# A linear-attention and gated-FFN kernel: k's product on GpSimd, paired score matmuls, one state multiply, and another order

## The chip, the cores and the metric

The kernel runs on one core of one Trainium2 chip. The metric is the device time of one execution in microseconds (us); the comparison uses the median over several runs. The engines are TensorE (PE, with its weight loads shown apart as PEld), VectorE (DVE), ScalarE (ACT), GpSimd (POOL) and SyncE (SP), which issues most of the DMAs.

## The reference

A recurrence over 768 steps for 4 batches and 8 heads of dimension 48, then an RMS norm and a gated feed-forward layer (384 to 1536 to 384) on all 3072 tokens.

```
state = zeros((B, H, D, D))                      # B, H, S, D = 4, 8, 768, 48
for t in range(S):
    cur = einsum('bhd,bhe->bhde', u[None] * kt, vt)
    y[:, :, t] = einsum('bhd,bhde->bhe', rt, state + cur)
    state = wt[:, :, :, None] * state + einsum('bhd,bhe->bhde', kt, vt)
x = y.transpose(0, 2, 1, 3).reshape(B * S, H * D)
xn = x / sqrt(mean(x * x, axis=-1) + 1e-06) * rms_g
g = xn @ w_gate
out = (g / (1 + exp(-g)) * (xn @ w_val)) @ w_out
```

## The kernel before, in words

The sequence is cut into six superblocks n = 0 to 5 of 128 steps; each has four pieces j = 0 to 3, one per batch. A piece fills the 128 partitions with its steps and has 384 columns, 8 heads of 48. The recurrence runs in chunked form: within a piece by masked score matrices, from one superblock to the next by a state.

One piece passes through these steps, which are Python functions of (n, j). `load_r`, `load_k`, `load_v`, `load_w` bring inputs (lines 213 and 226, on SP's queue). `ln` takes the logarithm of w (ScalarE). `cs_mm` forms cumulative sums of it by a matmul with a triangular mask into PSUM (L369), four one-column matmuls for the totals of the chunk, one per pair of heads (L372), and, in superblock 2, a second masked sum for k (L375). In superblocks 3 to 5 `cs_add` makes k's sum on VectorE from the first one (L380). Superblocks 0 and 1 share a wider load of w and have their own sums (L355 to L362). `exp_r` and `exp_k` take exponentials; they are in place in PSUM except in superblock 1, where they write SBUF. `w_tot` copies the exponentials of the totals to SBUF (L400). `r_mul` (L403) and `k_mul` (L408) multiply r and k by their factors on VectorE and write bf16. `rk_tr` transposes both: by PE and a ScalarE copy in superblocks 0 and 1 (`rk_pe`, L431), by one DMA transpose on SP's queue in 2 to 5 (L436). `q_mm` computes the scores of even heads (L449, partitions 0 to 47) and odd heads (L451, partitions 64 to 111) in alternating matmuls into two PSUM banks. `q_mask_e` masks the even half on VectorE (L456); `q_copy_o` copies the odd half on ScalarE (L460) and `q_mask_o` masks it on GpSimd (L467). `st_mm` (L477) and `st_new` (L483, L485) make the next state. `y_mm` (L494, L497) gives the output of the piece.

The diagonal term has steps of its own: `bonus_mul` is two GpSimd products (L414, L415), `bonus_sum` a VectorE reduction (L419), `bonus_v` a GpSimd product (L424), and `x_add` adds it to y (L502). `x_sq`, `x_rstd` and `xn_mul` form the norm (ScalarE; GpSimd L515 and L516 for the root; ScalarE L520). In superblocks 0 to 3 `xn_pe` and `xn_out` transpose it through PE (L531, L542); in 4 and 5 a DMA transpose (`xn_tr`, L525) and `xn_gain` (L546) do.

The feed-forward layer of superblock n then takes, for each of 12 slices f of the hidden dimension, `gate_mm` and `val_mm` (three matmuls of 128x512 each, L557, into the PSUM pools psA and psB), `silu` on ScalarE (L200, as all activations), `h_mul` on VectorE (L575), and for each batch `o_mm` (twelve matmuls, L620, into psQ), `o_out` (L627 on VectorE, L629 on ScalarE) and `out_dma` (L635).

`ORDER` is a list of some 1,090 steps, one word per step, such as `gate_mm.1.5`. The last lines of the kernel run through it and call the functions. Every engine executes its instructions in the order in which this list issues them, SP's queue included, so the list decides what stands behind what. While superblock n has its gate and val matmuls, the recurrence of n + 1 is woven between them. `warm` is a matmul on zeros with no reader, used in the first 30 us. PSUM has eight banks: two in psA, two in psB, four in psQ, each pool taken in turn.

Of the kernel before, what the change touches and what calls it, by code (L numbers as in the profile page):

```python
# [25 lines left out]
load_r.0.0 load_k.0.1 load_w.0.0 warm.15.0 warm.25.0 load_w.0.1 ln.0.0 warm.3.0 warm.14.0 warm.33.0 cs_mm.0.0 warm.17.0  # L26
warm.23.0 warm.28.0 load_v.0.0 load_w.0.3 cast_v.0.0 load_k.0.0 load_w.0.2 bonus_mul.0.0 load_r.0.1 bonus_mul.0.1
load_r.0.2 load_k.0.2 load_r.0.3 load_v.0.1 bonus_mul.0.2 ln.0.1 exp_r.0.0 r_mul.0.0 ln.0.3 exp_k.0.0 w_tot.0.0
k_mul.0.0 bonus_sum.0.0 warm.7.0 warm.6.0 cs_mm.0.1 exp_r.0.1 r_mul.0.1 load_k.0.3 bonus_mul.0.3 load_v.0.3 warm.32.0
warm.11.0 warm.24.0 warm.16.0 load_k.1.1 load_v.0.2 load_r.1.0 load_k.1.3 load_k.1.0 load_r.1.3 load_v.1.0 load_r.1.1  # L30
warm.2.0 warm.30.0 warm.10.0 warm.9.0 rk_pe.0.0 load_v.1.1 load_k.1.2 load_r.1.2 load_w.2.1 bonus_v.0.0 load_v.1.2
load_gv.0.1 load_w.2.0 load_v.1.3 st_mm.0.0 st_new.0.0 ln.0.2 exp_k.0.1 warm.31.0 k_mul.0.1 load_r.2.0 warm.21.0
load_k.2.1 load_w.2.2 load_v.2.1 load_k.2.0 rk_tr.0.0 cs_mm.0.2 exp_r.0.2 bonus_sum.0.1 w_tot.0.1 bonus_v.0.1
load_gv.0.0 r_mul.0.2 exp_k.0.2 k_mul.0.2 rk_pe.0.1 warm.8.0 rk_tr.0.1 q_mm.0.0 q_mask_o.0.0 cs_mm.0.3 warm.5.0
exp_r.0.3 r_mul.0.3 w_tot.0.2 exp_k.0.3 k_mul.0.3 load_w.2.3 load_k.2.2 load_r.2.1 rk_pe.0.2 warm.0.0 warm.12.0
q_mm.0.1 rk_tr.0.2 load_r.2.2 cs_mm.1.0 exp_r.1.0 warm.1.0 warm.20.0 warm.18.0 w_tot.0.3 q_mask_o.0.1 q_mask_e.0.1
rk_pe.0.3 warm.13.0 warm.26.0 warm.4.0 cast_v.0.1 exp_k.1.0 q_mask_e.0.0 y_mm.0.0 warm.22.0 warm.19.0 rk_tr.0.3
cast_v.0.2 cast_v.0.3 bonus_sum.0.2 bonus_sum.0.3 warm.27.0 x_add.0.0 warm.29.0 x_sq.0.0 load_r.2.3 r_mul.1.0 q_mm.0.2
q_mask_e.0.2 y_mm.0.1 cs_mm.1.1 x_rstd.0.0 exp_k.1.1 xn_mul.0.0 warm.35.0 x_add.0.1 q_mask_o.0.2 warm.34.0 q_mm.0.3
q_mask_e.0.3 x_sq.0.1 exp_r.1.1 x_rstd.0.1 load_k.2.3 y_mm.0.2 bonus_v.0.2 x_add.0.2 x_sq.0.2 xn_mul.0.1 x_rstd.0.2  # L40
xn_mul.0.2 q_mask_o.0.3 cs_mm.1.2 st_mm.0.3 st_mm.0.2 st_new.0.2 xn_pe.0.0 bonus_v.0.3 y_mm.0.3 x_add.0.3 load_gv.1.0
load_gv.1.1 bonus_mul.1.0 xn_out.0.0 xn_pe.0.1 xn_out.0.1 x_sq.0.3 x_rstd.0.3 xn_mul.0.3 xn_pe.0.2 xn_out.0.2 cs_mm.1.3
exp_r.1.3 exp_r.1.2 exp_k.1.3 xn_pe.0.3 st_new.0.3 k_mul.1.0 rk_pe.1.0 rk_tr.1.0 st_mm.0.1 xn_out.0.3 gate_mm.0.0
gate_mm.0.1 exp_k.1.2 q_mm.1.0 val_mm.0.1 k_mul.1.3 r_mul.1.3 silu.0.0 st_new.0.1 val_mm.0.0 rk_pe.1.3 q_mask_e.1.0
h_mul.0.0 k_mul.1.1 q_copy_o.1.0 silu.0.1 h_mul.0.1 gate_mm.0.2 silu.0.2 gate_mm.0.6 silu.0.6 val_mm.0.2 h_mul.0.2
bonus_sum.1.0 gate_mm.0.3 gate_mm.0.5 val_mm.0.3 silu.0.3 h_mul.0.3 cast_v.1.0 st_mm.1.0 gate_mm.0.9 st_new.1.0
silu.0.5 gate_mm.0.4 silu.0.9 r_mul.1.1 val_mm.0.5 h_mul.0.5 bonus_mul.1.3 gate_mm.0.7 rk_tr.1.3 cast_v.1.1 silu.0.4
val_mm.0.4 h_mul.0.4 st_mm.1.1 rk_pe.1.1 st_new.1.1 val_mm.0.9 val_mm.0.6 h_mul.0.6 r_mul.1.2 bonus_v.1.0 q_mask_o.1.0
y_mm.1.0 bonus_mul.1.1 k_mul.1.2 rk_tr.1.1 gate_mm.0.8 silu.0.8 silu.0.7 val_mm.0.7 h_mul.0.7 rk_pe.1.2 rk_tr.1.2
q_mm.1.1 q_copy_o.1.1 gate_mm.0.11 silu.0.11 load_wo.0.0 load_wo.2.0 q_mask_e.1.1 x_add.1.0 bonus_mul.1.2 load_wo.1.0  # L50
val_mm.0.8 h_mul.0.8 h_mul.0.9 q_mm.1.3 q_copy_o.1.3 q_mask_o.1.3 bonus_sum.1.3 q_mm.1.2 q_mask_e.1.2 q_copy_o.1.2
bonus_sum.1.1 gate_mm.0.10 val_mm.0.11 silu.0.10 val_mm.0.10 h_mul.0.10 bonus_sum.1.2 h_mul.0.11 q_mask_o.1.1 y_mm.1.1
x_sq.1.0 q_mask_o.1.2 cast_v.1.2 y_mm.1.2 bonus_v.1.1 x_add.1.1 o_mm.0.0 q_mask_e.1.3 ln.2.0 cs_mm.2.0 ln.2.1 cs_mm.2.1
bonus_v.1.2 x_add.1.2 o_out.0.0 out_dma.0.0 x_rstd.1.0 x_sq.1.1 cast_v.1.3 y_mm.1.3 st_mm.1.3 st_new.1.3 o_mm.0.1
bonus_v.1.3 x_rstd.1.1 x_add.1.3 exp_r.2.0 xn_mul.1.0 xn_pe.1.0 exp_k.2.1 k_mul.2.1 xn_mul.1.1 exp_r.2.1 w_tot.2.1
x_sq.1.2 x_rstd.1.2 r_mul.2.0 xn_out.1.0 w_tot.2.0 st_mm.1.2 st_new.1.2 o_mm.0.2 ln.2.2 cs_mm.2.2 x_sq.1.3 xn_mul.1.2
xn_pe.1.2 exp_k.2.0 k_mul.2.0 rk_tr.2.0 o_out.0.1 xn_pe.1.1 xn_out.1.1 xn_out.1.2 o_mm.0.3 exp_k.2.2 k_mul.2.2
load_v.2.0 r_mul.2.1 rk_tr.2.1 ln.2.3 x_rstd.1.3 exp_r.2.2 w_tot.2.2 xn_mul.1.3 xn_pe.1.3 xn_out.1.3 cs_mm.2.3
exp_r.2.3 r_mul.2.2 r_mul.2.3 w_tot.2.3 exp_k.2.3 k_mul.2.3 load_w.3.0 cast_v.2.1 st_mm.2.1 load_w.3.3 val_mm.1.1
gate_mm.1.1 silu.1.1 h_mul.1.1 o_out.0.2 load_v.2.2 rk_tr.2.3 load_v.4.3 rk_tr.2.2 load_v.2.3 load_k.3.1 load_r.3.1  # L60
o_out.0.3 out_dma.0.3 st_new.2.1 gate_mm.1.0 silu.1.0 val_mm.1.0 h_mul.1.0 bonus_mul.2.1 bonus_sum.2.1 gate_mm.1.5
silu.1.5 gate_mm.1.7 silu.1.7 val_mm.1.5 h_mul.1.5 bonus_mul.2.2 bonus_mul.2.0 bonus_v.2.1 gate_mm.1.3 silu.1.3
q_mm.2.0 q_mask_e.2.0 bonus_sum.2.2 q_mm.2.1 q_mask_e.2.1 gate_mm.1.2 silu.1.2 val_mm.1.2 h_mul.1.2 gate_mm.1.4
cast_v.2.0 st_mm.2.0 st_new.2.0 val_mm.1.3 h_mul.1.3 val_mm.1.4 gate_mm.1.6 bonus_mul.2.3 cast_v.2.2 st_mm.2.2
q_copy_o.2.1 bonus_sum.2.0 silu.1.4 h_mul.1.4 silu.1.6 q_copy_o.2.0 bonus_v.2.2 q_mask_o.2.0 q_mask_o.2.1 bonus_sum.2.3
cast_v.2.3 gate_mm.1.8 st_new.2.2 val_mm.1.7 gate_mm.1.9 h_mul.1.7 val_mm.1.9 y_mm.2.1 x_add.2.1 bonus_v.2.0 silu.1.9
h_mul.1.9 gate_mm.1.10 silu.1.10 y_mm.2.0 x_add.2.0 bonus_mul.3.1 val_mm.1.6 h_mul.1.6 q_mm.2.2 q_copy_o.2.2
q_mask_o.2.2 x_sq.2.0 q_mask_e.2.2 x_rstd.2.0 q_mm.2.3 q_mask_e.2.3 val_mm.1.8 val_mm.1.11 silu.1.8 h_mul.1.8
bonus_sum.3.1 bonus_v.2.3 q_copy_o.2.3 q_mask_o.2.3 load_r.3.0 load_k.3.0 bonus_mul.3.0 gate_mm.1.11 silu.1.11
h_mul.1.11 st_mm.2.3 y_mm.2.2 ln.3.0 val_mm.1.10 h_mul.1.10 o_mm.1.0 x_add.2.2 st_new.2.3 o_out.1.0 xn_mul.2.0 y_mm.2.3  # L70
x_add.2.3 cs_mm.3.0 xn_pe.2.0 cs_add.3.0 load_w.3.1 load_k.3.2 ln.3.1 cs_mm.3.1 cs_add.3.1 xn_out.2.0 out_dma.0.1
load_w.3.2 ln.3.2 x_sq.2.1 x_rstd.2.1 x_sq.2.2 load_k.3.3 out_dma.0.2 load_r.4.1 load_r.3.3 load_v.3.0 out_dma.1.0
load_v.3.2 load_r.3.2 exp_r.3.0 w_tot.3.0 bonus_sum.3.0 r_mul.3.0 ln.3.3 exp_k.3.1 exp_k.3.0 k_mul.3.0 rk_tr.3.0
exp_r.3.1 w_tot.3.1 r_mul.3.1 k_mul.3.1 rk_tr.3.1 o_mm.1.1 o_out.1.1 load_v.3.1 load_v.3.3 load_r.4.2 x_rstd.2.2
xn_mul.2.2 xn_mul.2.1 x_sq.2.3 cast_v.3.0 x_rstd.2.3 o_mm.1.2 o_out.1.2 cs_mm.3.3 cs_mm.3.2 cs_add.3.2 cs_add.3.3
xn_pe.2.1 xn_out.2.1 xn_pe.2.2 xn_out.2.2 bonus_mul.3.2 cast_v.3.2 exp_r.3.2 w_tot.3.2 r_mul.3.2 exp_k.3.3 xn_mul.2.3
exp_k.3.2 o_mm.1.3 o_out.1.3 xn_pe.2.3 xn_out.2.3 q_mm.3.0 q_copy_o.3.0 q_mask_o.3.0 k_mul.3.2 rk_tr.3.2 q_mask_e.3.0
exp_r.3.3 r_mul.3.3 w_tot.3.3 k_mul.3.3 bonus_sum.3.2 load_k.4.2 load_k.4.1 load_k.4.0 load_w.4.0 load_w.4.1 load_r.4.0
rk_tr.3.3 load_w.5.1 st_mm.3.0 st_new.3.0 bonus_mul.3.3 bonus_sum.3.3 bonus_v.3.1 bonus_v.3.0 gate_mm.2.0 silu.2.0
val_mm.2.0 h_mul.2.0 y_mm.3.0 gate_mm.2.7 q_mm.3.1 silu.2.7 x_add.3.0 gate_mm.2.4 gate_mm.2.1 silu.2.1 val_mm.2.4  # L80
val_mm.2.1 h_mul.2.1 st_mm.3.2 silu.2.4 q_mask_e.3.1 h_mul.2.4 gate_mm.2.5 gate_mm.2.3 cast_v.3.1 st_mm.3.1 val_mm.2.3
val_mm.2.7 h_mul.2.7 x_sq.3.0 x_rstd.3.0 xn_mul.3.0 silu.2.3 h_mul.2.3 st_new.3.2 silu.2.5 gate_mm.2.6 silu.2.6
cast_v.3.3 gate_mm.2.2 silu.2.2 val_mm.2.2 h_mul.2.2 bonus_mul.4.1 bonus_sum.4.1 bonus_v.3.3 val_mm.2.6 gate_mm.2.8
# [48 lines left out]
def kernel(  # L132
# [42 lines left out]

    def sel(s):
        return {(int(x[0]), int(x[1])) for x in s.split()}

    CAST_ACT = sel("00 01 02 03 10 11 12 13")
    EXPR_SB = sel("10 11 12 13")  # L180
    EXPK_SB = sel("10 11 12 13")
    WIN = (0, 1)
    Q_PAIR = ((4, 2),)
    OLD_DVE = (1, 2, 3, 4)
    ONE_SUM = (3, 4, 5)
    O_IN_A = ()
    XOUT_ACT = sel("")
# [484 lines left out]
```

## Time and profile before

| | us |
|---|---|
| median of 3 runs | 207.44 (207.34 to 208.61) |
| profiled execution, its own time | 208.67 |
| its span, first to last instruction | 206.9 |
| first gate matmul starts | 31.83 |
| last output matmul ends | 203.93 |

| what | instructions | busy us | mean ns |
|---|---|---|---|
| gate and val matmuls, L557 | 432 | 112.5 | 380, 385 |
| output matmuls, L620 | 300 | 49.4 | 320 |
| hidden product, L575, DVE | 72 | 48.6 | 686 |
| silu, L200, ACT | 72 | 42.1 | 598 |
| bonus products, L414 and L415, POOL | 48 | 48.0 | 999 |
| k's product from PSUM, L408, DVE | 20 | 10.8 | 546 |
| r's product from PSUM, L403, DVE | 20 | 10.8 | 545 |
| old state added, L483, DVE | 16 | 8.9 | 557 |
| state multiplied, L485, DVE | 40 | 14.1 | 354, 355 |
| second masked sum, L375, PE | 4 | 1.3 | 323 |
| totals, L372, PE | 64 | 3.9 | 164 |
| totals copied, L400, DVE | 16 | 2.4 | 152 |

The profile is of one execution. A matmul's duration holds its way through the array, so its mean is more than the distance from one start to the next; the same goes, less so, for VectorE and ScalarE. The granted clock of TensorE is 0.992 of full speed over the span; the only slice of the page below full is at about 31 to 36 us. The DMA engines are full over most of the first 60 us.

The page in 40 slices, each digit the busy share in tenths:

```
PE   1999969989999999999999999999999999999994
DVE  5169895789998899999879999998986676236521
ACT  2587998557997645889557968576976666064400
POOL 6098980390959379739776859738330464000000
PEclk9999997999999999999999999999999999999999
DMA  6999999999996999969989989982128401140013
```

### The profile page before, as it was taken

Reading aid. Unit: us, or ns where it says so; the run is one execution under the profiler, and the core shown is the slowest. Engines: PE = TensorE matmul, PEld = TensorE weight load, DVE = VectorE, ACT = ScalarE, POOL = GpSimd, SP = SyncE. Lnnn points to the kernel's source line nnn. Section 1 sums busy time; section 2 is a strip of 40 time slices with the busy share of each in tenths; the row PEclk is TensorE's granted clock in tenths of the full one; section 3 lists DMA queues with packets and bytes.
Section 4 is the critical chain, followed back from the end, with each engine's and each line's share of the span. In section 5 each row is a group of like instructions: output and inputs, shape, how many; then the busy total and the mean of one; then the engine's idle time right before and its main releaser. Section 6 shows DMA issues by size and latency. Waiting matters only on the chain.

```text
span 206.9 us, 4493 instructions
## 1 busy us (share of the span) xinstructions
PE 195.5 (94%) x1608; PEld 114.8 (55%) x1608; DVE 159.3 (77%) x324; ACT 138.1 (67%) x278; POOL 108.9 (53%) x170
## 2 busy tenths in 40 slices
PE   1999969989999999999999999999999999999994
PEld 1566545555665555665546665556555556555562
DVE  5169895789998899999879999998986676236521
ACT  2587998557997645889557968576976666064400
POOL 6098980390959379739776859738330464000000
PEclk9999997999999999999999999999999999999999
DMA  6999999999996999969989989982128401140013
GB/s 139 287 229 188 186 213 203 189 197 207 202 210 134 204 212 222 204 142 197 204 156 262 196 193 244 199 160 47 22 76 212 105 5 38 38 155 0 0 55 137
DMA packets 121566, 32.41 MB, mean 157 GB/s; under 512 B 116420, under 2 KB 120392, under 8 KB 121544
## 3 DMA queue, kind: packets, MB, share of 16 engines
q1 hardware_dynamic: 119504, 28.58, 64.4%
q0 software_dynamic: 2032, 3.54, 9.4%
q8 instruction: 12, 0.20, 0.4%
q14 instruction: 10, 0.08, 0.1%
q10 hardware_dynamic: 8, 0.00, 0.0%
HBM read 25.96 MB, written 4.72 MB: 148 GB/s over the span
## 4 chain that ended last, share of the span: by engine, by line
PE 50%; DVE 14%; DMA 9%; ACT 9%; POOL 6%; SPq 6%; issue 6%; DVEq 0%; POOLq 0%; ACTq 0%
PE ps_q L620 13%; PE ps_a L557 13%; PE ps_b L557 12%; DMA rt<-in_r_dram 7%; DVE ht L575 3%; SPq L213 3%; DMA vt<-in_v_dram 2%; DVE st L485 2%; PE ps_q L449 2%; ACT xn L520 2%; SPq L226 2%; PE ps_q L431 2%; POOL qts L467 1%; POOL ruk L415 1%; PE ps_q L333 1%
## 5 line engine op out<-in xcount | busy, mean ns | idle before, releaser
L200 ACT ACTIVATE sg<-ps_a 128x512 bf16<-128x512 f32 x72 | 42.1, 598 | 38.3 <-PE ps_a L557 27.9
L575 DVE TENSOR_TENSOR ht<-ps_b,sg 128x512 bf16<-128x512 f32 x72 | 48.6, 686 | 20.6 <-ACT sg L200 10.9
L557 PE MATMUL ps_b<-xnt,wv_sb 128*128 128x512 bf16 x216 | 56.5, 380 | 1.0 <-DVE ht L575 0.7
L557 PE MATMUL ps_a<-xnt,wg_sb 128*128 128x512 bf16 x216 | 56.0, 385 | 0.1
L620 PE MATMUL ps_q<-wo_sb,ht 128*128 128x384 bf16 (+1 forms) x300 | 49.4, 320 | 0.2 <-ACT ob L629 0.2
L620 PEld LDWEIGHTS <-ht 128*128 128x128 bf16 x300 | 28.2, 98 | 17.1 <-issue 0.2
L557 PEld LDWEIGHTS <-wg_sb 128*128 128x128 bf16 x216 | 23.4, 115 | 20.6 <-issue 1.6
L557 PEld LDWEIGHTS <-wv_sb 128*128 128x128 bf16 x216 | 22.9, 114 | 20.2 <-issue 2.6
L414 POOL TENSOR_TENSOR ruk<-rt,kt 128x384 f32<-128x384 f32 x24 | 24.0, 999 | 13.7 <-DVE rk L403 6.3
L424 POOL TENSOR_TENSOR ydiag<-vt,diag 128x384 f32<-128x384 f32 x24 | 20.0, 839 | 12.9 <-DVE diag L419 12.8
L415 POOL TENSOR_TENSOR ruk<-ruk,u_bc 128x384 f32<-128x384 f32 x24 | 24.0, 999 | 1.9
L467 POOL TENSOR_SCALAR_AFFINE_SELECT qts<-qts 128x512 bf16<-128x512 bf16 x20 | 12.4, 634 | 19.0 <-ACT qts L460 19.0
L456 DVE TENSOR_TENSOR qts<-ps_q,mask_lt 128x512 bf16<-128x512 f32 x24 | 16.2, 681 | 1.5 <-PE ps_q L451 1.4
L520 ACT ACTIVATE xn<-xb,rstd 128x384 bf16<-128x384 f32 x24 | 14.4, 611 | 3.8 <-POOL rstd L516 3.6
L502 DVE TENSOR_TENSOR xb<-ps_q,ydiag 128x384 f32<-128x384 f32 x24 | 13.2, 549 | 1.5 <-PE ps_q L497 1.4
L198 ACT ACT_TABLE_LOAD x10 | 12.8, 1283 | 1.8 <-PEq L656 1.6
L419 DVE TENSOR_REDUCE diag<-ruk 128x8 f32<-128x384 f32 x24 | 13.0, 544 | 1.1 <-POOL ruk L415 1.0
L403 DVE TENSOR_TENSOR rk<-rt,ps_a 128x384 bf16<-128x384 f32 x20 | 10.8, 545 | 3.6 <-ACT ps_a L200 3.5
L507 ACT ACTIVATE junk<-xb 128x384 bf16<-128x384 f32 x24 | 12.4, 517 | 1.6 <-DVE xb L502 1.3
L200 ACT ACTIVATE lw<-wt 128x384 bf16<-128x384 f32 (+1 forms) x20 | 11.0, 577 | 3.6 <-DMA wt<-in_w_dram 3.5
L515 POOL TENSOR_SCALAR rstd<-rstd 128x1 f32<-128x1 f32 x20 | 3.8, 190 | 16.5 <-ACT junk L507 15.6
L460 ACT CAST qts<-ps_q 128x512 bf16<-128x512 f32 x20 | 11.3, 585 | 1.0 <-PE ps_q L451 0.8
(83 smaller groups left out, 281.5 us busy)
## 6 DMA issues: line engine op xcount, KB each, us to landing
rt<-in_r_dram SPq DMA_DIRECT2D x24, 192.0 KB, 4.0
kt<-in_k_dram SPq DMA_DIRECT2D x24, 192.0 KB, 3.7
vt<-in_v_dram SPq DMA_DIRECT2D x24, 192.0 KB, 3.6
out_dram<-ob SPq DMA_DIRECT2D x23, 192.0 KB, 2.1
wt<-in_w_dram SPq DMA_DIRECT2D x16, 192.0 KB, 3.6
wt<-in_w_dram SPq DMA_DIRECT2D x4, 384.0 KB, 4.6
wo_sb<-in_moe_w_out_dram POOLq DMA_DIRECT2D x3, 384.0 KB, 7.1
wg_sb<-in_moe_w_gate_dram POOLq DMA_DIRECT2D x1, 768.0 KB, 10.0
```

The lines of the kernel that those rows point to most:

```text
L200: return nc.scalar.activation(**kw).ins
L414: nc.gpsimd.tensor_tensor(out=ruk[n, j], in0=inp["r", n, j], in1=inp["k", n, j], op=ALU.mult)
L415: nc.gpsimd.tensor_tensor(out=ruk[n, j], in0=ruk[n, j], in1=u_bc, op=ALU.mult)
L419: nc.vector.tensor_reduce(out=diag[n, j].rearrange("p h o -> p (h o)"), in_=ruk[n, j], axis=mybir.AxisListType.X, op=ALU.add)
L424: nc.gpsimd.tensor_tensor(out=ydiag[n, j], in0=inp["v", n, j], in1=diag[n, j].to_broadcast([128, H, D]), op=ALU.mult)
L456: nc.vector.tensor_tensor(out=qts[n, j][:, 0], in0=bank["q", n, j][0], in1=bc_mid(mask_lt, NP), op=ALU.mult)
L467: nc.gpsimd.affine_select(out=qts[n, j][:, 1], in_=qts[n, j][:, 1], compare_op=ALU.is_gt, fill=0.0, base=0, pattern=[[0, NP], [1, 128]], c ...
L502: nc.vector.tensor_tensor(out=xb[n, j], in0=bank.pop(("y", n, j)), in1=ydiag[n, j].rearrange("p h d -> p (h d)"), op=ALU.add)
L520: nc.scalar.activation(out=xn, in_=xb[n, j], func=AF.Copy, scale=rstd[n, j][:, 1:2])
L557: nc.tensor.matmul(ps, lhsT=units(ws, c, f), rhs=xnt[n][:, c, :], start=(c == 0), stop=(c == KC - 1))
L575: nc.vector.tensor_tensor(out=ht[n][:, f, :], in0=bank.pop(("v", n, f)), in1=bank.pop(("sg", n, f)), op=ALU.mult)
L620: nc.tensor.matmul(ps[:, cols], lhsT=ht[n][:, f, b * L:(b + 1) * L], rhs=wo_sb[:, f, cols], start=(f == 0), stop=(f == FC - 1))
```

## The change

Six things change together.

- `q_mm` in superblocks 2 to 5 issues the score matmuls of two batches in one step (before: one such pair, 4.2 with 4.3).
- `k_mul` in superblocks 2 to 5 runs on GpSimd; `exp_k` writes SBUF there, since GpSimd takes its operand from SBUF.
- `st_new` multiplies the whole tile of both heads of a pair in one instruction, by a factor that is zero off the diagonal blocks; `w_tot` writes that factor, with the help of a constant `half_of`, and now runs for superblock 1 as well.
- Superblock 2 forms k's sum by `cs_add` as 3 to 5 do, without the second masked matmul.
- Superblock 5 leaves out the four one-column matmuls for its totals, which no later state reads.
- `ORDER` is another list (1,092 steps), and the PSUM banks within the three groups of two, two and four are chosen by the last use that the list has for them, not in turn.

Functions that no step calls (`half`, `fc_half`, `gate_h`, `val_h`, `silu_h`, `h_h`) go away. The new list is left out here.

```diff
-    psA = ctx.enter_context(tc.tile_pool(name="psA", bufs=2, space=bass.MemoryType.PSUM))
-    psB = ctx.enter_context(tc.tile_pool(name="psB", bufs=2, space=bass.MemoryType.PSUM))
-    psQ = ctx.enter_context(tc.tile_pool(name="psQ", bufs=4, space=bass.MemoryType.PSUM))
+    psP = ctx.enter_context(tc.tile_pool(name="psP", bufs=1, space=bass.MemoryType.PSUM))
...
-    EXPK_SB = sel("10 11 12 13")
+    K_POOL = sel("20 21 22 23 30 31 32 33 40 41 42 43 50 51 52 53")
+    EXPK_SB = sel("10 11 12 13") | K_POOL
     WIN = (0, 1)
-    Q_PAIR = ((4, 2),)
+    Q_PAIR = ((2, 0), (2, 2), (3, 0), (3, 2), (4, 0), (4, 2), (5, 0), (5, 2))
     OLD_DVE = (1, 2, 3, 4)
-    ONE_SUM = (3, 4, 5)
+    ONE_SUM = (2, 3, 4, 5)
...
+    steps = [(x.split(".")[0], int(x.split(".")[1]), int(x.split(".")[2])) for x in ORDER.split()]
+    last_use, at = {}, [0]
+    for i, step in enumerate(steps):
+        for key in banks_of(*step):
+            last_use[key] = i
+    rings = {"a": [[-2, 0], [-2, 1]], "b": [[-2, 0], [-2, 1]], "q": [[-2, 0], [-2, 1], [-2, 2], [-2, 3]]}
+    taken = [9]
+
+    def psum(ring, key, shape, dtype=FP32):
+        slots = rings[ring]
+        k = min((x for x in range(len(slots)) if slots[x][0] < at[0]), key=lambda x: slots[x])
+        taken[0] += 1
+        slots[k] = [last_use.get(key, -1), taken[0]]
+        return psP.tile(shape, dtype, name="ps_" + ring + "uvxz"[k])
...
+    half_of = small.tile([128, 2], FP32)
+    nc.vector.memset(half_of, 0.0)
+    nc.vector.memset(half_of[0:PD, 0:1], 1.0)
+    nc.vector.memset(half_of[PD:128, 1:2], 1.0)
...
     def cs_mm(n, j):
...
+        last = n == NSB - 1
         nc.tensor.matmul(a[:, NP:NP + DM].rearrange("p (h d) -> p h d", h=H), lhsT=mask_lt, rhs=rhs,
-                         start=True, stop=False)
-        for q in range(NP):
+                         start=True, stop=last)
+        for q in range(0 if last else NP):
             nc.tensor.matmul(a[:, q:q + 1], lhsT=pair(lwj, q), rhs=ones_col,
                              start=False, stop=(q == NP - 1))
...
     def w_tot(n, j):
-        wcol[n, j] = small.tile([128, NP], FP32, name="wcol", bufs=12)
-        nc.vector.tensor_copy(out=wcol[n, j], in_=bank["cs_r", n, j][:, 0:NP])
+        wcol[n, j] = small.tile([128, NP, 2], FP32, name="wcol", bufs=12)
+        nc.vector.tensor_tensor(out=wcol[n, j], in0=bank["cs_r", n, j][:, 0:NP].unsqueeze(2).to_broadcast([128, NP, 2]),
+                                in1=bc_mid(half_of, NP), op=ALU.mult)
...
     def k_mul(n, j):
-        nc.vector.tensor_tensor(out=rk[:, n % 2, j, 1, :, 0:D], in0=inp["k", n, j],
+        eng = nc.gpsimd if (n, j) in K_POOL else nc.vector
+        eng.tensor_tensor(out=rk[:, n % 2, j, 1, :, 0:D], in0=inp["k", n, j],
...
     def st_new(n, j):
...
-        for p0, c0 in ((0, 0), (PD, D)):
-            nc.vector.tensor_tensor(
-                out=new[p0:p0 + D, :, c0:c0 + D], in0=ps[p0:p0 + D, :, c0:c0 + D],
-                in1=wc[p0:p0 + D, 0:NP].to_broadcast([D, NP, D]), op=ALU.mult)
+        nc.vector.tensor_tensor(out=new.rearrange("p q (c d) -> p (q c) d", c=2),
+                                in0=ps.rearrange("p q (c d) -> p (q c) d", c=2),
+                                in1=wc.rearrange("p q c -> p (q c)").unsqueeze(2).to_broadcast([128, 2 * NP, D]),
+                                op=ALU.mult)
```

## The prediction

> **What bounds the kernel now.** I read the page's busy times first, then sums over stretches that I cut at the first and last matmuls of each superblock's gate/val and output phases, then groups by shape, then the chain that ended last. The busy times name TensorE:
>
> ```profile
> PE 195.5 (94%) x1608; PEld 114.8 (55%) x1608; DVE 159.3 (77%) x324; ACT 138.1 (67%) x278; POOL 108.9 (53%) x170
> ```
>
> A busy PE is not a PE at its peak, so I measure its pace on the chain. The columns are start, duration in us, and work:
>
> ```profile
> 31.83 2.24 PE ps_a L557 x6
> ...
> 172.75 7.80 PE ps_q L620 x48
> ...
> 190.91 1.29 PE ps_a L557 x6
> ...
> 196.09 7.84 PE ps_q L620 x60
> ```
>
> Undisturbed, a gate or val matmul takes 1.29/6 = 0.215 us and an output matmul 7.80/48 = 0.163. From the first gate matmul (31.83) to the last output matmul (196.09 + 7.84 = 203.93) there are 172.1 us. In them lie 432 gate/val matmuls (92.9), 276 output matmuls of full and 24 of half width (276 x 0.163 + 24 x 0.083 = 46.8), and the small matmuls of the recurrence. Those I take from the chain's and the timeline's start-to-start times: 20 y steps at 0.38, 16 state steps at 0.17, 16 cumulative sums at 0.26 to 0.42, 12 transposes of xn at 0.17, 3 of rk at 0.45, 20 score steps (L449/L451) at 0.30: 24 us. That leaves 172.1 - 92.9 - 46.8 - 24 = about 8 us in which PE waited. Ahead of it is a head of 31.8 us, behind it 3.0 us of last copy and store.
>
> Where could the 8 us come from? Stretches, busy us of PE, PEld, DVE, ACT, POOL:
>
> ```profile
> 31.80:55.70 23.90, 23.22 (x185) 12.89 (x183) 18.93 (x36) 17.91 (x31) 10.67 (x15) 0.96 1.06 199
> ...
> 65.10:84.80 19.70, 19.48 (x158) 10.64 (x156) 17.94 (x36) 12.39 (x23) 14.48 (x21) 1.00 1.02 215
> 84.80:95.90 11.10, 10.81 (x105) 7.00 (x104) 10.97 (x27) 10.27 (x25) 6.57 (x12) 1.00 0.73 157
> 95.90:120.50 24.60, 24.20 (x201) 13.85 (x200) 22.85 (x48) 18.12 (x37) 19.71 (x31) 1.00 1.01 202
> ...
> 172.75:203.90 31.15, 31.15 (x180) 18.18 (x178) 12.31 (x22) 11.13 (x22) 1.48 (x4) 1.00 0.17 58
> ```
>
> VectorE is 91 to 99% busy from 65 to 120: in the middle it is as near its limit as PE. From 172.75 on nothing but PE counts, and the same 31.15 us of PE work stand there afterwards, so no gain can come from there. The chain agrees: between 59 and 81 it runs on VectorE. From 97 to 109 it leaves the compute engines altogether:
>
> ```profile
> 97.58 0.39 SPq L436
> ...
> 102.02 4.92 DMA rt<-in_r_dram
> 106.94 0.07 issue
> 107.01 1.00 POOL ruk L414
> ```
>
> A load issued behind a transpose on SP's queue arrives late and holds GpSimd. The same shape returns at 115.84 and 133.98.
>
> **The change, part by part.** Durations of one instruction stand in the groups by shape (busy us, mean ns, idle before):
>
> ```profile
> L414 POOL TENSOR_TENSOR ruk<-rt,kt 128x384 f32<-128x384 f32 x24 | 24.0, 999 | 13.7 <-DVE rk L403 6.3 <-DMA kt<-in_k_dram 3.7 <-DMA rt<-in_r_dram 3.6
> ...
> L485 DVE TENSOR_TENSOR st<-ps_q,wcol 48x192 bf16<-48x192 f32 x32 | 11.3, 354 | 0.6
> L408 DVE TENSOR_TENSOR rk<-kt,ps_b 128x384 bf16<-128x384 f32 x20 | 10.8, 546 | 1.4 <-ACT ps_b L200 1.3
> ```
>
> *Matmuls left out.* Superblock 2 loses four 128x384 sums with the second mask, 0.16 each (start to start), and superblock 5 four groups of totals at 0.10 (0.08 on the chain, 0.10 to the next start): 4 x 0.16 + 4 x 0.10 = 1.0 us, all on PE inside the 172.1.
>
> *Score matmuls in pairs.* The diff suggests seven new pairs, but the old order already has most of them back to back on PE, with only other engines' steps between (2.0 and 2.1; 2.2 and 2.3; 3.2 and 3.3; 5.0 and 5.1; 5.3 and 5.2). Superblocks 2 to 5 have ten uninterrupted groups now and eight afterwards. What a group costs beside its matmuls shows at 48.15: eight transposes at 0.056 should end at 48.60, the first score matmul starts at 48.77; the last pair's turn ends at 49.00, the next gate matmul starts at 49.10. That is 0.27 per break, and 2 x 0.27 = 0.5 us.
>
> *k's product to GpSimd.* 16 instructions of 546 ns leave VectorE, whose starts in a row are 0.46 to 0.48 apart: 16 x 0.475 = 7.6 us. On GpSimd the nearest rows are the same shape without the bf16 output (999) and a product with a broadcast operand (839), with starts up to 1.08 apart: 16 x 1.0 = 16 us, between 13.4 and 17.3. GpSimd goes from 108.9 to 125 of its 207. I cost that at nothing: per superblock it has 4 x (2 x 0.999 + 0.839 + 0.634 + 0.502 + 0.739) = 18.9 us of work now and 22.9 after, in about 30 us of PE work, and the score step stands 10 to 18 us of PE work behind its cumulative sum, against some 6.5 us of chain between them (sum and exponential 0.5 each, product 1.0, transpose 1.2 to issue and 3.2 to land). The exponential of k goes to SBUF for it: 493 ns against 472 in the rows, 0.3 us in all on ScalarE, which has room. If the cover is gone, the price is that of the second rival. One row speaks for the move beyond the count: with both inputs in SBUF, VectorE's r product took 796 ns against 545 from PSUM. Superblocks 2 to 5 keep no VectorE product with both inputs in SBUF.
>
> The Trainium skill speaks against this part: "GPSIMD Engine Reference", section "Engine selection", puts elementwise products of two tensors on VectorE and calls GpSimd about twice as slow. The rows agree on the ratio (999 to 546, 1.8), but the rule leaves out which engine is full; by the rule alone the product would stay and its 7.6 us of relief would be zero, by the rows of the stretches the slower engine has the room.
>
> *One state multiply.* Two products of 48 partitions, 0.71 together (0.35 and 0.36 on the chain), become one of 128x384 out of PSUM. The trace has no such instruction; its bounds are 354 ns (half as many elements per row) and 681 (the 128x512 mask product), and the nearest row, the add of the same tile, has 557, or 0.48 start to start. I take that: 20 x (0.71 - 0.48) = 4.6 us off VectorE, between 0.6 and 7.2.
>
> *Added on VectorE.* Four sums for superblock 2's k at 0.48 (1.9 us) and four more totals at 0.15 (0.6). The total now writes eight columns in place of four, priced as before.
>
> VectorE's balance is 7.6 + 4.6 - 1.9 - 0.6 = 9.7 us less, to 150. That is not time off the end: only PE's waits are. Of the 8 us, I give 2.0 to this and to the loads. The new order puts the loads of r and k of superblocks 3 to 5 at 8 to 33 us of PE work ahead of their first use, where the old one has r.3.0, k.3.0, r.5.0, k.5.0 and k.5.1 directly ahead of it. The bounds are 0 (PE waits for something else) and 4 (half; 2 to 3 us of the rest lie at 31 to 47, where gate/val starts up, which the change hardly touches).
>
> *The head.* Both orders hold the same 18.3 us of PE work and the same ScalarE work up to the last xn. The old one has ScalarE wait 1.3 us at 8.27 for a load of v ahead of its second logarithm; the new one puts that cast behind three exponentials, but lets the first w land behind one more large load (the 384 KB loads take 4.6 us to land). I take 0.5 us gained, between 1.3 gained and 1.5 lost.
>
> *Bank choice.* PSUM banks are picked by the last use written in the order rather than in turn; it adds no instruction, and its effect lies inside PE's waits. The loads and stores keep number and size; SP's 16 transposes of rk now wait for GpSimd in place of VectorE, with loads queued behind them.
>
> The sum: 1.0 + 0.5 + 2.0 + 0.5 = 4.0 us. The profiled execution took 208.67 (span 206.9 and 1.8 around it), 1.2 over the runs' median of 207.44. Off its own time that is 204.7, off the median **203.4**.
>
> **Rivals.** *PE's waits stay.* If VectorE's load was hidden under PE anyway, only the removed matmuls and breaks count: 207.44 - 1.5 = 205.9. For it: PE is 97% busy or more in every stretch. Against: the chain's VectorE pieces.
>
> *GpSimd becomes the bound (slower).* Counted in the new order with the rows' durations, GpSimd has 28.6 us of work between the first output matmuls of superblocks 0 and 1, where PE has 28.8 (now 25.2 against 29.4). It works strictly in turn and waits for VectorE's sums and ScalarE's copies; its best present 10 us window in the middle is 82% busy (80 to 90). At that share 28.6 us last 34.9, 6.1 longer than PE: 207.44 - 1.5 + 6.1 = 212.0. It decides once GpSimd passes 90% there, so that superblock 2's products, queued behind two-instruction bonus products, hold up SP's transposes and the loads behind them. Against: much of its work is for the next superblock and can slip.
>
> **How the numbers follow.** Forecast 0.68, waits stay 0.17, GpSimd bound 0.15. The low end takes the upper bounds of waits and head: 207.44 - 1.5 - 4 - 1.3 = 200.6. The high end reaches half-way into the second rival: 207.44 - 1.5 + 3 = 208.9. Outside lie some 0.05 below and 0.12 above. One per cent, about what a measurement can tell from no change, is 2.1 us: faster means under 205.4. The forecast gives 0.64 to faster and 0.04 to the same, the first rival 0.06 and 0.11, the second all of its 0.15 to slower.
>
> **What would show it.** Gate matmuls starting by 31.3; 168.6 us from there to the last output matmul; VectorE near 150 and GpSimd near 125 us busy; the state multiply near 0.55 us; no load of r or k on the chain after 60. I am wrong if the product on GpSimd takes well over 1.1 us, if GpSimd is over 90% busy from 60 to 100, if score matmuls wait for transposes, or if the head grows.

## The result, and the profile after

The changed kernel took 205.42 us (median of four runs, 204.31 to 208.0) against 207.39 beside it: ratio 0.986, 95% interval 0.982 to 0.990. Repeated later, it took 204.46 (six runs, 202.93 to 206.27) against 207.95: 0.980 (0.975 to 0.984). Executions over 1.5% above the fastest of their kernel, here those of 208.0 and 206.27, are in the medians and ranges but not in the ratios. The profiled execution took 204.31 (span 202.6), 4.4 less than the one profiled before.

The busy times, from the page (engine, busy us, share of the span, instructions):

```profile
PE 189.0 (93%) x1570; PEld 113.0 (56%) x1588; DVE 153.0 (75%) x299; ACT 137.2 (68%) x278; POOL 125.4 (62%) x186
```

The weight loads count the matmuls: 1608 before, 1588 now, the 4 second sums and 16 totals that went. GpSimd has grown by the 16 us of k's product.

Groups by shape (busy us, mean ns, idle before it):

```profile
L443 POOL TENSOR_TENSOR rk<-kt,ek 128x384 bf16<-128x384 f32 x16 | 15.9, 1001 | 3.8 <-ACT ek L229 3.8
L437 DVE TENSOR_TENSOR rk<-rt,ps_av 128x384 bf16<-128x384 f32 x10 | 5.5, 546 | 0.0
L519 DVE TENSOR_TENSOR st<-ps_qx,wcol 128x384 bf16<-128x384 f32 x8 | 4.5, 557 | 0.2
L437 DVE TENSOR_TENSOR rk<-rt,er 128x384 bf16<-128x384 f32 x4 | 3.8, 958 | 0.0
L443 DVE TENSOR_TENSOR rk<-kt,ek 128x384 bf16<-128x384 f32 x4 | 3.5, 881 | 0.0
L581 DVE TENSOR_SCALAR xnt<-xnt,gT 128x512 bf16<-128x512 bf16 x6 | 3.2, 567 | 1.1 <-DMA xnt<-xn 1.1
```

k's product takes 1001 ns, the state multiply 557. The last three rows are dearer than before (958, 881 and 567 ns for 796, 609 and 346), and all three read nothing but SBUF; of that more at the end.

The stretches from the first gate or val matmul of one superblock to that of the next (start:end, length; then busy us and instructions of PE, PEld, DVE, ACT, POOL; granted clock; DMA share; GB/s):

```profile
31.52:62.12 30.60, 30.38 (x269) 18.55 (x273) 29.19 (x58) 25.51 (x52) 20.32 (x29) 1.00 1.05 203
62.12:91.14 29.02, 28.78 (x247) 17.25 (x249) 26.41 (x55) 21.79 (x45) 23.00 (x34) 1.00 1.07 196
91.14:120.00 28.86, 28.70 (x247) 17.25 (x248) 25.11 (x51) 21.62 (x44) 25.26 (x36) 1.00 1.11 208
120.00:148.17 28.17, 27.66 (x219) 16.01 (x220) 22.27 (x42) 21.16 (x43) 21.97 (x34) 1.00 0.72 156
148.17:176.03 27.86, 26.24 (x197) 15.08 (x201) 18.30 (x34) 15.72 (x32) 13.43 (x22) 1.00 0.29 73
```

The same stretches were 33.46, 30.65, 29.28, 29.09 and 26.28 us long before. So the kernel gained 2.9, 1.6, 0.4 and 0.9 us in the first four (some 1 us of the 2.9 is a lower clock in the execution before), and lost 1.6 in the fifth; the head (31.63 to 31.52) and the last stretch changed by 0.1 at most. The 31.63 is the timeline's start of the first gate matmul; the 31.83 given earlier is where the chain's piece begins.

The chain of waits has changed too. This is a piece of it after the change, at the start of superblock 1's gate/val phase (start, us, work):

```profile
60.17 0.95 POOL rk L443
61.12 0.95 POOL ruk L449
62.08 0.04 issue
62.16 1.00 POOL ruk L450
63.16 0.46 POOL vb L373
63.66 0.33 PE ps_qx L512 x4
63.99 0.65 PE ps_av L592 x3
```

No load of r or k is on it any more. In its place GpSimd works without a pause, k's product among its instructions, and PE's state matmul waits for v's cast behind it. That wait is short: the gate matmuls ahead of it start at 62.77 and take 0.65 to the next start, so PE stands still for some 0.2 us. From there to 132 the chain runs on PE alone, where before it ran on VectorE from 59 to 81 and over loads and GpSimd from 97. The fifth stretch loses its time at its start, on the same chain:

```profile
144.89 2.31 DMA xnt<-xn
147.20 0.04 DVEq L581
147.24 0.05 issue
147.28 0.17 DVE xnt L581
147.45 0.58 issue
148.03 0.55 DVE ps_bv L414
148.59 1.36 DVE xnt L581 x2
```

The transposed norm lands at 147.2, and on VectorE one of superblock 5's sums stands between the three gains that the gate and val matmuls wait for. The gains themselves have become longer there as well (last section).

### The profile page after: what moved, and what is told of

Its sections match the earlier page's. It is cut to its first block, busy times and chain, and to the rows that moved or that the text cites. A ratio compares the mean times of both kernels' runs of the same rounds, so it can differ in the third digit from the quotient of the medians.

```text
span 202.6 us, 4425 instructions
## 1 busy us (share of the span) xinstructions
PE 189.0 (93%) x1570; PEld 113.0 (56%) x1588; DVE 153.0 (75%) x299; ACT 137.2 (68%) x278; POOL 125.4 (62%) x186
## 2 busy tenths in 40 slices
DMA packets 121566, 32.41 MB, mean 160 GB/s; under 512 B 116420, under 2 KB 120392, under 8 KB 121544
## 4 chain that ended last, share of the span: by engine, by line
PE 68%; ACT 10%; DVE 8%; POOL 6%; issue 4%; DMA 1%; POOLq 0%; DVEq 0%
PE ps_av L592 10%; PE ps_au L592 9%; PE ps_bu L592 9%; PE ps_bv L592 9%; PE ps_qv L624 5%; PE ps_qu L624 4%; PE ps_qx L624 3%; PE ps_qz L624 3%; DVE ht L610 2%; ACT junk L542 2%; DVE rk L437 2%; ACT rkT L475 1%; POOL rstd L551 1%; DMA xnt<-xn 1%; POOL ruk L450 1%
## 5 line engine op out<-in xcount | busy, mean ns | idle before, releaser
L229 ACT ACTIVATE sg<-ps_av 128x512 bf16<-128x512 f32 x38 | 22.8, 600 | 23.0 <-PE ps_av L592 16.2
L592 PEld LDWEIGHTS <-wv_sb 128*128 128x128 bf16 x216 | 23.0, 114 | 20.9 <-issue 2.0
L592 PEld LDWEIGHTS <-wg_sb 128*128 128x128 bf16 x216 | 23.2, 114 | 19.0 <-DVE wcol L433 0.2
L610 DVE TENSOR_TENSOR ht<-ps_bu,sg 128x512 bf16<-128x512 f32 x37 | 25.4, 686 | 9.4 <-PE ps_bu L592 8.9
L592 PE MATMUL ps_bu<-xnt,wv_sb 128*128 128x512 bf16 x108 | 29.7, 380 | 1.8 <-DVE xnt L581 1.7
L610 DVE TENSOR_TENSOR ht<-ps_bv,sg 128x512 bf16<-128x512 f32 x35 | 24.0, 687 | 9.1 <-ACT sg L229 5.4
L592 PE MATMUL ps_av<-xnt,wg_sb 128*128 128x512 bf16 x110 | 30.6, 380 | 0.2
L592 PE MATMUL ps_bv<-xnt,wv_sb 128*128 128x512 bf16 x98 | 28.0, 381 | 0.5 <-DVE xnt L577 0.2
L592 PE MATMUL ps_au<-xnt,wg_sb 128*128 128x512 bf16 x98 | 27.4, 379 | 0.3
L229 ACT ACTIVATE sg<-ps_au 128x512 bf16<-128x512 f32 x34 | 20.4, 600 | 7.3 <-PE ps_au L592 3.6
L443 POOL TENSOR_TENSOR rk<-kt,ek 128x384 bf16<-128x384 f32 x16 | 15.9, 1001 | 3.8 <-ACT ek L229 3.8
L624 PE MATMUL ps_qv<-wo_sb,ht 128*128 128x384 bf16 (+1 forms) x96 | 15.9, 316 | 0.0
```

The costliest lines, as they stand in the source:

```text
L229: return nc.scalar.activation(**kw).ins
L443: eng.tensor_tensor(out=rk[:, n % 2, j, 1, :, 0:D], in0=inp["k", n, j], in1=bank["cs_k", n, j][:, 0:DM].rearrange("p (h d) -> p h d", h=H) ...
L592: nc.tensor.matmul(ps, lhsT=units(ws, c, f), rhs=xnt[n][:, c, :], start=(c == 0), stop=(c == KC - 1))
L610: nc.vector.tensor_tensor(out=ht[n][:, f, :], in0=bank.pop(("v", n, f)), in1=bank.pop(("sg", n, f)), op=ALU.mult)
L624: nc.tensor.matmul(ps[:, cols], lhsT=ht[n][:, f, b * L:(b + 1) * L], rhs=wo_sb[:, f, cols], start=(f == 0), stop=(f == FC - 1))
```

## The experiments

Twelve runs, on three chips; "ratio" is to the kernel before on the same chip, which took 207.83 us beside e1, e2, e5 and e7, 208.24 beside e3, e4, e6 and e9, and 207.95 beside e0, e8, e10 and e11.

| run | us, median (runs) | ratio, 95% interval |
|---|---|---|
| e1, parts in the old order | 225.59 (224.55 to 225.96) | 1.081 (1.073 to 1.088) |
| e9, the same, k on VectorE | 211.37 (210.06 to 214.72) | 1.013 (1.008 to 1.019) |
| e10, as e9, banks in turn | 217.0 (215.88 to 218.12) | 1.042 (1.037 to 1.046) |
| e6, new order, banks in turn | 217.84 (217.5 to 218.1) | 1.046 (1.042 to 1.051) |
| e2, new order, no relief | 214.67 (214.38 to 215.7) | 1.030 (1.023 to 1.037) |
| e3, new order, k on VectorE | 212.56 (211.02 to 214.41) | 1.019 (1.013 to 1.025) |
| e4, new order, two multiplies | 207.67 (206.88 to 209.95) | 0.999 (0.995 to 1.003) |
| e5, k's product twice | 215.61 (215.2 to 216.95) | 1.036 (1.027 to 1.044) |
| e11, one batch's scores at a time | 204.97 (203.65 to 205.87) | 0.983 (0.979 to 0.988) |
| e7, gains first | 207.45 (203.1 to 210.56) | 0.981 (0.968 to 0.994) |
| e8, gains and squares first | 205.74 (204.99 to 207.93) | 0.989 (0.984 to 0.994) |
| e0, the changed kernel again | 204.46 (202.93 to 206.27) | 0.980 (0.975 to 0.984) |

**Parts or order (e1, e2).** Theory: the parts free VectorE and leave out matmuls, and the order adds the loads' lead. Rival: the order alone, or the parts alone, has the gain. e1 keeps the old list, with only the steps added that the parts need:

```diff
-    Q_PAIR = ((2, 0), (2, 2), (3, 0), (3, 2), (4, 0), (4, 2), (5, 0), (5, 2))
+    Q_PAIR = ((4, 2),)
-ORDER: the new list
+ORDER: the list of before, w_tot.1.j behind exp_r.1.j, cs_add.2.j behind cs_mm.2.j
```

> All new parts in the old order: the old list with the new totals of superblock 1 and the sums for k of superblock 2 put behind the steps that they need; score matmuls paired as before. Removed matmuls are 1.0 us. Theory that the parts bring the gain by relief of VectorE: 204.0 to 205.5, that is, at least two thirds of the changed kernel's gain of 3 us. Rival, that the order brings it: 206.4 (only the removed matmuls) up to 209, since the old list puts loads directly ahead of their use and now also makes transposes wait for GpSimd products.

It was far worse than any theory allowed. The chain in its superblock 1 (start, us, work):

```profile
69.49 0.41 ACT ek L231
69.90 0.07 issue
69.97 0.99 POOL rk L445
70.96 0.46 POOL vb L375
71.41 0.04 issue
71.46 0.48 PE ps_qu L514 x4
71.93 1.28 PE ps_bv L594 x3
73.21 1.22 PE ps_av L594 x3
```

The old list puts the state matmul directly ahead of the first val matmul, and both its inputs now come from GpSimd, a product and a cast in a row. PE's last transpose of the norm starts at 67.57, its last four totals at 67.91; then PE stands still for 3.3 us, and the gate and val work behind the state matmul with it. The new list has a val and a gate matmul there first.

e2 keeps the new list and takes the relief of VectorE away:

```diff
-        eng = nc.gpsimd if (n, j) in K_POOL else nc.vector
+        eng = nc.vector
...
-        last = n == NSB - 1
+        last = False
...
-        nc.vector.tensor_tensor(out=new.rearrange("p q (c d) -> p (q c) d", c=2),
...
+        for c, (p0, c0) in enumerate(((0, 0), (PD, D))):
+            nc.vector.tensor_tensor(
+                out=new[p0:p0 + D, :, c0:c0 + D], in0=ps[p0:p0 + D, :, c0:c0 + D],
+                in1=wc[p0:p0 + D, :, c:c + 1].to_broadcast([D, NP, D]), op=ALU.mult)
```

> The new order with VectorE's relief undone: k's product on VectorE (both inputs in SBUF), two state multiplies of 48 partitions, and superblock 5's totals back (0.4 us of TensorE). VectorE gets 13 us or more of its work back. Relief theory: 2 to 4 us slower than the changed kernel, so 206.5 to 208.5. Order theory: 0.4 to 1 us slower, 205 to 206.

It was slower than before. The new list does not stand on its own: taking the relief away from it costs 9 to 10 us (214.7 against the changed kernel's 205.4 and 204.5), not the 2 to 4 expected. Neither half has the gain.

**Which relief (e3, e4).** e3 is the first hunk of e2 alone, e4 the last.

> The changed kernel with k's product of superblocks 2 to 5 back on VectorE, reading r-like from SBUF (16 x about 0.88 us added to VectorE, 16 x 1.0 taken from GpSimd), all else as after. Theory 'relief' (VectorE's load is what makes PE wait in superblocks 1 to 3): VectorE to about 166 us busy, PE's waits up by most of the 9 us that the run without any relief showed: 210 to 214 us. Rival 'the state multiply carries it': 206 to 208. Rival 'GpSimd was the late engine after the change': no slower than after, 204 to 206.

> The changed kernel with the state multiply as two products of 48 partitions again (0.71 us in place of 0.56 each time, by the profiles), all else as after. Theory 'relief': it has 4.6 of about 12 us of VectorE's relief by the prediction's prices, by the measured ones 16 x 0.15 = 2.4 us; some of it on the path in superblocks 1 to 3: 206.5 to 209 us. Rival 'hidden': under 206.3.

Both fit the theory of relief, for the new list. k's product on VectorE costs 7 to 8 us (0.033 and 0.039 of ratio against the two measurements of the changed kernel), the second multiply 3 to 4 (0.013 and 0.019). e3 overstates: its product reads SBUF, where the one before read PSUM, and it takes longer, as the groups by shape of e3 show:

```profile
L443 DVE TENSOR_TENSOR rk<-kt,ek 128x384 bf16<-128x384 f32 x20 | 16.7, 837 | 0.6 <-DMA kt<-in_k_dram 0.5
L437 DVE TENSOR_TENSOR rk<-rt,ps_au 128x384 bf16<-128x384 f32 x10 | 5.5, 546 | 0.5 <-ACT ps_au L229 0.5
```

So about 16 x (837 - 546) = 4.7 us of VectorE's load in e3 were never there before (2.9 by the 729 ns that the same row has in e2).

**Is GpSimd's share covered (e5)?** The prediction costed the 16 us at nothing. e5 issues each product twice, the same values into the same place:

```diff
+        if (n, j) in K_POOL:
+            eng.tensor_tensor(out=rk[:, n % 2, j, 1, :, 0:D], in0=inp["k", n, j], ...
```

> The changed kernel with k's product on GpSimd issued twice (the same values), 16 us more on GpSimd. If GpSimd has cover, as the forecast costed it: within 0.7 us of the changed kernel. If GpSimd is at its limit from 50 to 130 us (it shows 9.77 of 10 us busy from 60 to 70 and from 90 to 100): 3 to 8 us slower, 208 to 213.

The cover is used up: another 16 us on GpSimd cost 10 to 12 (ratio 1.036 for 0.986 and 0.980), more than the 3 to 8 expected. The page's shares of the chain in e5:

```profile
PE 41%; POOL 39%; DVE 5%; ACT 5%; issue 4%; SPq 3%; DMA 2%; POOLq 0%; DVEq 0%
```

After the change itself GpSimd has 6% of the chain, as before it.

**The bank choice (e6, e9, e10).** e6 is the changed kernel with one word different:

```diff
-        k = min((x for x in range(len(slots)) if slots[x][0] < at[0]), key=lambda x: slots[x])
+        k = min((x for x in range(len(slots)) if slots[x][0] < at[0]), key=lambda x: slots[x][1])
```

> The changed kernel with PSUM banks taken in turn (by when they were last given out) in place of by their last use, all else as after. Theory 'the bank choice is no part of the gain': 204.5 to 206.5 us. Rival 'a bank taken in turn is one whose last reader is late': PE waits for ScalarE's and VectorE's reads of the gate and val banks, 208 to 214, and the waits of gate and val matmuls name such a reader.

Of the parts undone alone in the new list this costs most: 12 to 14 us (ratio 1.046 for 0.986 and 0.980; 217.84 to 205.42 in medians). The rival held, and one kind of reader comes on top that it did not name. From the list of PE's waits in e6 (us in total, times, longest):

```profile
PE ps_bu L592 <- DVE ht L610: 3.5, 3, 1.7
PE ps_qu L624 <- DVE st L519: 1.8, 1, 1.8
PE ps_qv L512 <- DVE st L519: 1.3, 1, 1.3
PE ps_bv L592 <- DVE ht L610: 0.9, 2, 0.7
```

Gate and val matmuls (L592) wait 5.6 us in all for the reader of a gate or val bank: 4.4 for VectorE's hidden product (ht), 1.2 for ScalarE's silu. Matmuls into the other four banks wait 4.9, 3.3 of it for VectorE's new state (st). In the changed kernel all such waits on that list make 0.5 us, in the kernel before 1.5. e6's chain shows one of them, ahead of superblock 0's output matmuls:

```profile
60.07 0.40 DVE ob L631
60.47 0.08 issue
60.55 0.55 DVE xb L537
61.09 0.48 DVE ps_qu L518
61.58 0.02 issue
61.60 0.57 DVE st L519
62.17 0.04 issue
62.21 2.11 PE ps_qu L624 x12
```

The next bank in turn is ps_qu, which still holds a state. VectorE comes to it only behind an output copy and an add, so PE's twelve output matmuls (all their inputs there) stand from 60.05 to 62.21. Picked by last use, they go to a bank that the list has emptied earlier.

e9 is e1 with `K_POOL` empty (k's product on VectorE out of PSUM, as before); e10 is e9 with the edit of e6.

> The changed kernel's functions with the order of before (as the run that took 225.6 us), but k's product of superblocks 2 to 5 on VectorE out of PSUM as before; the state multiply in one, the one-sum form of superblock 2, no last totals and the bank choice stay. Theory 'the product on GpSimd is what the old order can't carry': 204 to 208 us, the waits of GpSimd for the exponential and of ScalarE for the norm's scale gone. Rival 'the other parts or the bank choice break the old order': 215 to 226 us.

> The old order with the state multiply in one, the one-sum form of superblock 2 and no last totals, k's product on VectorE out of PSUM (as the run that took 211.4 us), but PSUM banks in turn in place of by their last use. Theory 'an order fits the bank choice it was found with': the old order loses 12 us the other way, so this is 204 to 208 us, at least 3 under 211.4. Rival 'picking by last use is better for any order': 213 us or more. Third, 'the bank choice matters in the new order alone': 210 to 213.

Of e1's loss of 18 us, k's product on GpSimd is 14 (225.6 to 211.4), the largest effect of one edit here: the old list cannot carry it. The rest is not explained: the old list with the other parts stays 3 us above the kernel before, between the two ranges expected. e10 gives no sign that a list prefers the choice it was found with: picking by last use is better by 5.6 us in the old list too. e10 differs from the kernel before only in the smaller parts (and in that a bank still held in the list is passed over) and is 9 us slower; whether superblock 2's sum, superblock 1's totals (both put into the old list by hand) or something else does that was not tried. Its trace points at the banks again: the waits of PE for a bank's reader make 8.8 us in e10, for 1.5 in the kernel before.

**Scores in pairs (e11).** The second batch's score matmuls are issued by a step of their own again, directly ahead of their first reader:

```diff
-    Q_PAIR = ((2, 0), (2, 2), (3, 0), (3, 2), (4, 0), (4, 2), (5, 0), (5, 2))
+    Q_PAIR = ()
-ORDER: the new list
+ORDER: the new list, q_mm.n.1 and q_mm.n.3 ahead of the first of their q_mask_e, q_copy_o (n = 2 to 5)
```

> The changed kernel with the score matmuls of superblocks 2 to 5 for one batch at a time again, the second batch's directly ahead of its first reader: twelve uninterrupted groups on PE in place of eight. Theory of the prediction (a break costs 0.27 us): 4 x 0.27 = 1.1 us over the changed kernel beside it. Rival 'a break costs nothing, since weights load beside the matmuls before': within 0.5 of it. Third, 'scores taken later hold up VectorE, ScalarE and GpSimd behind them': 3 us or more over it.

0.5 us above e0 (ratios 0.983 and 0.980, intervals overlapping): the expected 1.1 can't be told from nothing, and 3 us or more are excluded. The pairs are a small part of the gain, if any.

**A better version (e7, e8, e0).** Both edits go for the 1.6 us lost in the fifth stretch (1.05 in e0's profile): e7 moves the sum and exponential of superblock 5's last k behind the gains, e8 also moves two squares ahead of a logarithm and its table load.

```diff
-xn_gain.4.0 cs_add.5.3 exp_k.5.3 xn_gain.4.2 xn_gain.4.1
+xn_gain.4.0 xn_gain.4.2 xn_gain.4.1 cs_add.5.3 exp_k.5.3
-cast_v.5.0 ln.5.1 cs_mm.5.1 st_new.4.3 bonus_sum.5.2 x_rstd.4.1 x_sq.4.2 x_sq.4.3   (e8 only)
+cast_v.5.0 x_sq.4.2 x_sq.4.3 ln.5.1 cs_mm.5.1 st_new.4.3 bonus_sum.5.2 x_rstd.4.1   (e8 only)
```

> The changed kernel with the last sum for k of superblock 5 put behind the three gain products of superblock 4 on VectorE, so that the first val matmul of superblock 4 does not wait for it. That wait is 1.4 us at 148.6 in the changed kernel. If the sum holds the gains: 0.5 to 1.1 us faster than the changed kernel. If the transposes' landing holds them: within 0.2 us.

> The changed kernel with the start of superblock 4's gate/val phase cleared: in the order, superblock 5's last k sum (cs_add.5.3, exp_k.5.3) behind xn_gain.4.1, and x_sq.4.2 and x_sq.4.3 ahead of ln.5.1 and its table load. Theory 'the 1.97 us that PE waits in that step are VectorE's and ScalarE's order': 203.5 to 205 us, 0.7 to 2 under the changed kernel beside it, the step from superblock 3's to superblock 4's gate/val phase 27.2 or less (28.16 after). Rival 'those waits come back one step later, or superblock 5's scores get late': within 0.7 of the changed kernel or over it.

> The changed kernel itself, for comparison on the same chip with the three beside it: 205 to 206.3 us by the runs so far, a ratio to the kernel before of 0.982 to 0.990.

e7's runs spread over 7 us and settle nothing. e8 was 1.3 us over e0 beside it: the step to superblock 4's phase became longer (29.16 for 27.54 in e0's profile, 28.16 in the first), and the one after it no shorter (27.37 for 27.33). In its trace PE stands 0.70 and 0.59 us ahead of superblock 5's sums at 142.13 and 143.05 for the logarithm that the squares were put ahead of: the wait came back, as the rival had it, but a step earlier and not later. None of the twelve is shown to beat the changed kernel.

## Why the prediction was right, and where it was not

*The bound and the sum.* Right. From the first gate matmul to the start of the last output matmul the profile went from 172.0 to 167.8 us, 4.2 less where the terms for matmuls, breaks and waits made 3.5; some 1 us of the difference is the dip of the clock in the execution profiled before (its first six gate matmuls took 2.24 us for 1.29). e0's profile, which has such a dip too (clock 0.83 from 30 to 40), comes to the same 167.8. The two medians, 205.4 and 204.5, are 1.0% and 0.5% over the forecast. One product of the prediction is off: 276 x 0.163 + 24 x 0.083 is 47.0, not 46.8, which takes 0.2 from the 8 us of waits.

*Matmuls left out (1.0 us).* The count is as said, 20 fewer; not measured alone. *Breaks (0.5 us).* Four breaks came to 0.5 us, where the price of 0.27 makes 1.1, both within the spread of the runs: the price is neither shown nor excluded.

*State multiply.* 0.557 was taken from the add of the same tile; it measured 0.554 to 0.558. Two multiplies in its place cost 3 to 4 us in the new list.

*k's product on GpSimd.* 16 x 1.0 us and GpSimd at 125 were met exactly (15.9, 125.4). "Costed at nothing" was right for these 16 us and wrong as a statement about the room: from 60 to 100 GpSimd is 33.7 of 40 us busy, 84%, but in two of the four windows it is full (columns as in the stretches; GpSimd's busy time is the last before the clock):

```profile
60.00:70.00 10.00, 9.87 (x64) 5.31 (x64) 7.86 (x18) 6.30 (x11) 9.77 (x13) 1.00 1.02 204
...
90.00:100.00 10.00, 9.89 (x78) 5.73 (x78) 7.32 (x16) 6.62 (x11) 9.77 (x13) 1.00 1.24 199
```

The chain runs over it from 55.7 to 63.6. The sign named for the second rival (over 90%) was seen in half of the stretch. That rival's mechanism is real, and its point lies between the 16 us that the change adds and the 32 of e5; in the old order it lies below 16 (e1).

*VectorE to 150.* It went to 153. The products from PSUM and the state kept their prices; rows that read SBUF alone became dearer: the gain of the norm by 6 x (567 - 346) = 1.3 us, superblock 1's r and k products by 4 x (958 - 796) + 4 x (881 - 609) = 1.7. The sizes are those of one execution: e0's profile, of the same kernel, has 504, 798 and 746 ns, which makes 1.5 in all, and VectorE at 152.

*PE's waits (2.0 of 8 us).* 4.2 less 1.5 for matmuls and breaks and 1 for the clock leaves 1.7; by e0's profile, with a dip on both sides, it is 2.7. So the size was right, and its account half right. VectorE and the loads did leave the chain, as the prediction had it, though the stretch in which most of the loads stood on it (95.74 to 125.02) gained only 0.4 us. But the prediction put the bank choice "inside PE's waits" without a price. That is the step that failed, and that the sum came out all the same is in part luck. Undone alone, the bank choice costs 12 to 14 us, k's product 7 to 8, the state multiply 3 to 4: together over 20, for a change that brought 2.0 and 3.5. They are not terms of a sum. Each one taken from a list that was made with it lets PE wait for whatever that list had just in time; the removal of a part from the new kernel is not the price of adding it to the old one (e1 and e9 show that: there the parts cost time). How the 2 to 3 us divide between relief, loads and banks stays open.

*The head (0.5 us).* The gate phase starts at 31.52, not by 31.3; the term is nothing (31.41 and 31.70 in e8 and e11, 32.41 in e0).

*The first rival (waits stay).* Its 205.9 lies near the first median, but it is 0.993 of 207.44, above both intervals (at most 0.990 and 0.984; the latter is 204.2 of 207.44). e3 and e4 show that VectorE's load is not hidden in the new list; for the old list no run shows it alone.

## What to carry to other kernels

In a kernel whose order is written out, a part moved to another engine and the order belong together: predict the pair, and do not read the price of a part from taking it out of the finished pair. Look at which bank a matmul group writes as closely as at its inputs: in e6 twelve matmuls with all inputs ready waited two microseconds for a bank whose old tile VectorE had yet to read. An engine at 62% over the span can be full where it counts; read the 10 us windows before costing anything on it at zero.

## What the runs showed of the chip

*VectorE beside GpSimd.* The gain of the norm reads and writes SBUF in bf16. The groups by shape of the kernel before and of e5 (k twice on GpSimd):

```profile
L546 DVE TENSOR_SCALAR xnt<-xnt,gT 128x512 bf16<-128x512 bf16 x6 | 1.7, 346 | 3.8 <-DMA xnt<-xn 3.8
```

```profile
L585 DVE TENSOR_SCALAR xnt<-xnt,gT 128x512 bf16<-128x512 bf16 x6 | 3.5, 624 | 0.7 <-DMA xnt<-xn 0.7
```

The changed kernel has 567 ns (504 in e0). These means mix two kinds, as its line L581 shows when it is asked for superblock 4 and superblock 5 apart (ns: least, median, most; first and last start):

```profile
L581 DVE TENSOR_SCALAR xnt<-xnt,gT x3: 449/827/1078, 147.3 to 148.9; 128x512 bf16<-128x512 bf16 x3
L581 DVE TENSOR_SCALAR xnt<-xnt,gT x3: 346/348/352, 175.0 to 175.6; 128x512 bf16<-128x512 bf16 x3
```

GpSimd is at work from 146.97 to 150.89, beside the first three, and idle beside the others. In the fourteen profiles 56 of the 84 gains have no GpSimd instruction beside them and take 337 to 355 ns; the other 28 take 349 to 1092. Superblock 1's r and k products from SBUF behave alike: without GpSimd beside them they take 539 to 558 ns, as much as the product with one operand in PSUM, whose groups stayed at 544 to 549 in every run. So the 796 ns that the prediction held against a product from SBUF, and e3's 837, come from GpSimd's work beside it and not from SBUF as such. Superblock 4's gains stayed beside GpSimd in e7 and e8 too: in e8 they took 354, 349 and 1092 ns. The Trainium skill ("SBUF — State Buffer", section "Who interferes with whom") has this: VectorE and GpSimd share a pair of SBUF ports, which VectorE needs for a second SBUF input or in its two-port modes, and not otherwise. The rows agree; in which mode the gain ran, no row says. It also bears on the rule weighed in the prediction: GpSimd's product is 1.8 times VectorE's from PSUM (1001 to 546), but only 1.2 times VectorE's from SBUF beside a busy GpSimd (837 in e3; 1.4 by e2's 729).

*The clock after a wait.* In e1 PE stands idle for a third of a 10 us window, and the granted clock of the next is lower (windows, columns as above):

```profile
60.00:70.00 10.00, 6.59 (x58) 4.16 (x56) 7.14 (x18) 6.05 (x16) 4.08 (x8) 1.00 0.64 141
70.00:80.00 10.00, 8.54 (x50) 4.22 (x50) 5.02 (x12) 4.77 (x8) 8.81 (x11) 0.83 0.97 205
```

The chain lines of e1 above show it: its val and gate matmuls at 71.93 and 73.21 take 1.28 and 1.22 us for three, where 0.65 is usual. So this long wait of PE cost some 1.2 us more than its length. It is no rule here: PE is busy for 8.01 us from 60 to 70 in e5 and for 7.55 in e2, and the clock stays at 1.00 after it.
